# Weight blocks for the product scheme kept in device memory instead of being added up again, with earlier sums of y

## Chip, cores and metric

The kernel runs on one core of one Trainium2 chip. The metric is the device time of one execution in microseconds (us). Three runs of the kernel before gave 550.37, 550.64 and 551.04 us.

## What is computed

Two sequences of 768 tokens (8 heads of 64) go through a local-plus-summary attention; its output, 1536 x 512, goes through a maxout layer and then through a bilinear layer. All of it is f32.

```
a = softmax([scores in a window of 16 tokens | scores against 24 block maxima of k])
x = a @ [v | block means of v]                      # 1536 x 512
h = maximum(maximum(x @ w1, x @ w2), x @ w3)        # 1536 x 768
y = h @ w_out                                       # 1536 x 512
out = ((y @ w_a) * (y @ w_b)) @ w_out2              # 1536 x 1536 inside, 1536 x 512 out
```

## The kernel before

**Chunks and operands.** The tokens are four chunks of 384: chunks 0 and 1 are the first sequence, 2 and 3 the second. f32 accuracy comes from splitting every operand into a rounded high part and a low part (fp32r); `mm3` (L532) makes one product of three matmuls, high x high, low x high, high x low. A matmul here is 128 x 128 weights against 128 x 384 tokens. One block of weights is 128 x 512 (four such tiles), 24 matmuls for one pair of chunks.

**Weights.** A block arrives as 512 KB of 64-bit numbers (`w_load`, L434, issued by SyncE into the tiles `w64`), is rounded to f32 in the tile `w32` (`w_round`: ScalarE L454 and L456, VectorE L458 and L459, GpSimd L460) and split into the tile `wt` (`w_split` and `w_parts`: ScalarE L464 the high part, VectorE or GpSimd L465 the low part). `weights()` calls these steps ahead of use; `W64` and `ERA0` are numbers of load tiles and set how far ahead the loads go. The `w32` block is freed once it is split.

**The order of the program.** Attention of the first sequence, its maxout with the first 18 weight blocks (`ph`, evacuated by `evac`), its second product `layer2` (`py`, giving `y` by `halves`) with the attention of the second sequence woven in (`TURNS` says between which steps), then `pair1()`: the maxout of the second sequence. `pair1` takes pairs of column blocks (f, m), nine in all. Two at the start and one at the end are `plain` (eight products of 12 matmuls each, `ph`). The six between are made two at a time by `products()`, a scheme that forms a 2 x 2 block product from seven products instead of eight (`PRODUCTS`; PSUM tiles `hb`, `hg`, `hd`). It wants sums and differences of the blocks of weights, `s`, and of x, `xs`. `x_sums` makes those of x (GpSimd `xr<-x` L592, then VectorE and ScalarE). `w_sums(f, m)` makes those of the weights, six times: the `w32` blocks are gone, so GpSimd first adds high and low part of two blocks to full blocks `rc`

```
        for r, w in ((r0, w0), (r1, w1)):
            G.tensor_tensor(r, w[:, 0], w[:, 1], ALU.add)
        s12, s34 = sums4(*(r[:, o:o + 256] for r in (r0, r1) for o in (0, 256)))
```

then VectorE makes four 128 x 256 sums (`sums4`, L471 to L474) and ScalarE and GpSimd split them (L464, L465 `wt<-s`). `result` evacuates the products on VectorE: `pt<-hd,s` and the like (L633), `pt<-pt` (L635, a maximum of two SBUF tiles), `pt<-hb,pt` and `pt<-ph,pt` (L640). `layer2` of chunks 2 and 3 follows (`py<-hg`), and then layer 3 (`qb`, `qg`, `qd`; for both sequences by the same seven products) and layer 4 (`po`).

**Sums of y.** Layer 3 wants sums of y as well. `sums_of` makes them; for the first sequence that is 11 VectorE instructions of 128 x 768 (`yt<-y,yt` L745 and `yd<-y` L749, with `yt<-y` on ScalarE, L744). They are called at the steps `SUMS` of `pair1`. The first loads of layer 3's weights have to wait for a tile of h (the gate, `GATE`): GpSimd copies a column of it into each load tile (L433), and the load comes behind that; their rounding begins with `psw<-w` (L454) and `w<-psw` (L458). In layer 3, `ca<-qb,m` (L803) is VectorE's evacuation of a product.

**What sets the order.** SyncE issues its DMAs in the order of the code. The rows of the other engines are ordered by a scheduler from the order of the code and from pins (`behind_marks`, `behind_all`) that hold chosen work behind chosen evacuations. Every engine works its rows off in order. `XSUMS`, `WSUMS` and `ASK` say at which steps of `pair1` the sums of x and of the weights are called.

## Time and profile before

| | |
|---|---|
| median of 3 runs | 550.64 us |
| the profiled execution | 549.45 us |
| its span | 547.2 us |
| granted TensorE clock | 1.00 in every stretch, the 2.4 GHz level |
| TensorE matmuls busy | 534.0 us, 98% of the span, 3328 |
| VectorE (DVE) busy | 422.2 us, 77% |
| ScalarE (ACT) busy | 284.6 us, 52% |
| GpSimd (POOL) busy | 245.9 us, 45% |

The span is read as one long row of matmuls: what TensorE (PE) does not spend on them is 13 us, and the question at each place is what it waits for there. PEld is the loading of weights into TensorE, which shows waits most plainly. Rows give a start and a duration in us, and in brackets the idle time before with the instruction that ended it.

### The profile page before, as it was taken

Reading aid. Unit: us, or ns where it says so; the run is one execution under the profiler, and the core shown is the slowest. Engines: PE = TensorE matmul, PEld = TensorE weight load, DVE = VectorE, ACT = ScalarE, POOL = GpSimd, SP = SyncE. Lnnn points to the kernel's source line nnn. Section 1 sums busy time; section 2 is a strip of 40 time slices with the busy share of each in tenths; the row PEclk is TensorE's granted clock in tenths of the full one; section 3 lists DMA queues with packets and bytes.
Section 4 is the critical chain, followed back from the end, with each engine's and each line's share of the span. In section 5 each row is a group of like instructions: output and inputs, shape, how many; then the busy total and the mean of one; then the engine's idle time right before and its main releaser. Section 6 shows DMA issues by size and latency. Waiting matters only on the chain.

```text
span 547.2 us, 9042 instructions
## 1 busy us (share of the span) xinstructions
PE 534.0 (98%) x3328; PEld 506.3 (93%) x3328; DVE 422.2 (77%) x863; ACT 284.6 (52%) x692; POOL 245.9 (45%) x207
## 2 busy tenths in 40 slices
PE   7899999999999999999989999999999999999997
PEld 7789999999999999989989989989998998998986
DVE  5798985885439677699999997985997798574464
ACT  4699775676533342567667645633544543340130
POOL 3479997642239577544334342521621442230120
PEclk9999999999999999999999999999999999999999
DMA  8998334375100000232311241132122121000014
GB/s 297 356 278 294 123 116 151 110 223 165 38 1 1 2 0 1 106 97 107 116 48 68 78 153 40 40 115 78 38 78 78 40 77 40 1 0 1 0 49 183
DMA packets 17132, 51.82 MB, mean 95 GB/s; under 512 B 2112, under 2 KB 2752, under 8 KB 17088
## 3 DMA queue, kind: packets, MB, share of 16 engines
q1 hardware_dynamic: 17088, 51.25, 28.0%
q8 instruction: 26, 0.43, 0.3%
q14 instruction: 18, 0.15, 0.1%
HBM read 48.09 MB, written 3.15 MB: 94 GB/s over the span
## 4 chain that ended last, share of the span: by engine, by line
PE 80%; DVE 9%; POOL 4%; issue 2%; ACT 1%; DMA 1%; DVEq 0%; POOLq 0%; ACTq 0%
PE ph L532 17%; PE qb L532 16%; PE py L532 9%; PE qg L532 8%; PE po L843 6%; PE po L844 6%; PE po L842 6%; PE qd L532 4%; PE ps L261 3%; PE psv L318 2%; PE pst L299 2%; POOL wt L465 1%; DVE yt L745 1%; DVE yd L749 1%; DVE w L459 1%
## 5 line engine op out<-in xcount | busy, mean ns | idle before, releaser
L460 POOL TENSOR_TENSOR w<-w,w 128x512 int32<-128x512 int32 x60 | 85.3, 1431 | 140.5 <-DVE w L459 79.9
L532 PE MATMUL qb<-yt,wt 128*128 128x384 f32 x576 | 109.9, 336 | 1.7 <-DVE ca L803 1.3
L532 PE MATMUL ph<-x,wt 128*128 128x384 f32 x576 | 107.2, 338 | 0.0
L532 PEld LDWEIGHTS qb<-yt,wt 128*128 128x128 f32 x576 | 101.0, 188 | 3.5 <-DVE ca L803 1.6
L532 PEld LDWEIGHTS ph<-x,wt 128*128 128x128 f32 x576 | 99.1, 188 | 0.3
L810 POOL TENSOR_TENSOR t<-t,ca 128x384 f32<-128x384 f32 x36 | 43.7, 1226 | 67.5 <-DVE t L809 67.3
L532 PE MATMUL qg<-yt,wt 128*128 128x384 f32 x288 | 57.8, 335 | 0.5 <-DVE yt L745 0.5
L856 DVE TENSOR_TENSOR acc<-po,acc 128x512 f32<-128x512 f32 (+1 forms) x61 | 40.7, 678 | 22.3 <-PE po L844 22.2
L843 PE MATMUL po<-wt,hg 128*128 128x512 f32 (+1 forms) x146 | 56.6, 387 | 0.0
L844 PE MATMUL po<-wt,hg 128*128 128x512 f32 (+1 forms) x146 | 56.5, 387 | 0.0
L842 PE MATMUL po<-wt,hg 128*128 128x512 f32 (+1 forms) x146 | 56.5, 387 | 0.0
L532 PE MATMUL py<-hg,wt 128*128 128x384 f32 x288 | 54.0, 340 | 1.1 <-DVE pt L640 1.1
L532 PEld LDWEIGHTS qg<-yt,wt 128*128 128x128 f32 x288 | 50.6, 188 | 0.8 <-DVE yt L745 0.8
L532 PEld LDWEIGHTS py<-hg,wt 128*128 128x128 f32 x288 | 49.5, 188 | 1.6 <-DVE pt L640 1.4
L536 ACT ACTIVATE hg<-t 128x384 fp32r<-128x384 f32 x60 | 30.8, 521 | 34.7 <-POOL t L810 28.7
L268 ACT ACTIVATE s<-s,nm 128x120 f32<-128x120 f32 x96 | 36.9, 387 | 20.5 <-DVE nm L267 20.4
L456 ACT ACTIVATE w<-w 128x512 int32<-128x512 uint32 x60 | 39.4, 671 | 4.7 <-DMA w<-wall 4.7
L454 ACT ACTIVATE w<-w 128x512 f32<-128x512 f32 x30 | 20.3, 675 | 41.2 <-DMA w<-wall 41.1
L464 ACT ACTIVATE wt<-w 128x512 fp32r<-128x512 f32 (+1 forms) x60 | 34.7, 583 | 12.9 <-POOL w L460 11.9
L286 POOL TENSOR_TENSOR s<-s,r 128x720 f32<-128x720 f32 x16 | 22.2, 1390 | 42.6 <-DVE r L284 36.0
L465 DVE TENSOR_TENSOR wt<-w,wt 128x512 fp32r<-128x512 f32 (+1 forms) x44 | 33.7, 768 | 1.5 <-ACT wt L464 1.3
L537 DVE TENSOR_TENSOR hg<-t,hg 128x384 fp32r<-128x384 f32 x48 | 34.2, 722 | 0.9 <-ACT hg L536 0.8
(115 smaller groups left out, 990.1 us busy)
## 6 DMA issues: line engine op xcount, KB each, us to landing
w<-wall SPq DMA_DIRECT2D x60, 512.0 KB, 3.4
qv<-qt SPq DMA_DIRECT2D x15, 384.0 KB, 6.1
row<-kt SPq DMA_DIRECT2D x8, 416.0 KB, 3.6
full<-vt SPq DMA_DIRECT2D x8, 384.0 KB, 6.2
out<-acc SPq DMA_DIRECT2D x11, 256.0 KB, 2.0
qv<-vwin SPq DMA_DIRECT2D x12, 192.0 KB, 5.3
qv<-vwin SPq DMA_DIRECT2D x12, 96.0 KB, 5.0
qv<-qt SPq DMA_DIRECT2D x1, 256.0 KB, 4.5
```

Of the source, the lines that this page charges most:

```text
L268: A.activation(s[:, a], s[:, a], AF.Exp, bias=nm[:, a:a + 1], scale=-1.0, accum_out=sm[:, a:a + 1])
L456: A.activation(lw.bitcast(I32), lw, AF.Copy, scale=2.0 ** -29)
L460: G.tensor_tensor(w.bitcast(I32), w.bitcast(I32), lw.bitcast(I32), ALU.add)
L464: A.activation(w[:, 0], r, AF.Copy)
L465: eng.tensor_tensor(w[:, 1], r, w[:, 0], ALU.subtract)
L532: ins = T.matmul(ps, w[:, i, o:o + P], x[:, j], start=first and n == 0, stop=last and n == 2, skip_group_check=more).ins
L537: ins = eng.tensor_tensor(dst[:, 1], src, dst[:, 0], ALU.subtract).ins
L810: G.tensor_tensor(t, t, cs[c, f], ALU.mult)
L842: T.matmul(ps, g[:, 0], w[:, 0], start=(f == 0), stop=False)
L843: T.matmul(ps, g[:, 0], w[:, 1], start=False, stop=False)
L844: ins = T.matmul(ps, g[:, 1], w[:, 0], start=False, stop=(f == 1)).ins
L856: V.tensor_tensor(acc[c, i][:, cols_], ps, acc[c, i][:, cols_], ALU.add)
```

## The change

The twelve 128 x 512 blocks that `w_sums` rebuilds are instead written from `w32` to device memory when they are rounded (`spill`, a DMA by SyncE ahead of the next block's split), and loaded back from there into `rc` by SyncE. GpSimd's twelve adds go. Some numbers move with it: fewer load tiles (`W64` 6 to 4, `ERA0` 10 to 8), two instead of one for one pool of attention tiles (`FB`), the sums of y of the first sequence at steps 32, 36, 40, 44 instead of 40, 43, 46, 49 (`SUMS`), the sums of x and of the weights one to three steps later (`XSUMS`, `WSUMS`, `ASK`), and the attention of the second sequence ending one step of the first product's order sooner (`TURNS`).

```diff
--- before.py
+++ after.py
@@ -53,15 +53,16 @@
-W64, W32, WBUFS, QB, FB, SM, GB, BANKS = (6, 3), (4, 3), (24, 10), 4, (9, 1), 2, (12, 9), (2, 2, 1, 2, 2)
-GATE, ROOM, SUMS, EARLY34 = (2, 1), 16, (40, 43, 46, 49), 6
-PLAIN, XSUMS, WSUMS, WS, PT, MAX_G, LO_G, ASK = (2, 1), (2, 4), (5, 7), 8, 7, False, True, (0, 2)
-RING, LEAD, TURN, ERA0, ASKS, AHEAD, PRE, TURNS = 8, 5, (11, 2, 4), 10, (3, 4, 5, 7, 9), (4, 1), 3, ((6, N1 - 6, 6, 4, 4), (24, 34), (34, 43))
+W64, W32, WBUFS, QB, FB, SM, GB, BANKS = (4, 3), (4, 3), (24, 10), 4, (9, 2), 2, (12, 9), (2, 2, 1, 2, 2)
+GATE, ROOM, SUMS, EARLY34 = (2, 1), 16, (32, 36, 40, 44), 6
+PLAIN, XSUMS, WSUMS, WS, PT, MAX_G, LO_G, ASK, RC = (2, 1), (3, 5), (7, 8), 8, 7, False, True, (1, 3), 2
+SPILL = {3 * (2 * (j // 3) + i) + j % 3 for j in range(PLAIN[0], 9 - PLAIN[1]) for i in range(2)}
+RING, LEAD, TURN, ERA0, ASKS, AHEAD, PRE, TURNS = 8, 5, (11, 2, 4), 8, (3, 4, 5, 7, 9), (4, 1), 3, ((6, N1 - 6, 6, 4, 4), (24, 33), (33, 42))
@@ -93,6 +94,7 @@
     acc_p = ctx.enter_context(tc.tile_pool(name="acc", bufs=B * NT))
     sm_p = ctx.enter_context(tc.tile_pool(name="sm", bufs=SM))
     mo_p = ctx.enter_context(tc.tile_pool(name="mo", bufs=2))
+    spill_p = ctx.enter_context(tc.tile_pool(name="spill", bufs=1, space=bass.MemoryType.DRAM))
     ps_s = ctx.enter_context(tc.tile_pool(name="ps_s", bufs=BANKS[0], space=PSUM))
     ps_t = ctx.enter_context(tc.tile_pool(name="ps_t", bufs=BANKS[1], space=PSUM))
     ps_v = ctx.enter_context(tc.tile_pool(name="ps_v", bufs=BANKS[2], space=PSUM))
@@ -474,9 +476,14 @@
         V.tensor_tensor(s34[:, 256:512], a12, s12[:, 256:512], ALU.subtract)
         return s12, s34
+    spilled, spill = {}, []
     def w_split(q):
         kind, n, i = kinds[q]
         eng = V if SPLIT_DVE[era(q)][q % 3] else G
+        if q in SPILL:
+            spilled[q] = spill_p.tile([P, 512], F32, tag=f"spill{q}", name="spill")
+            spill.append((spilled[q], w32_t[q]))
         if kind in ("w", "o"):
             w_t[q] = w_parts(w32_t.pop(q), eng, "w" if kind == "w" else "w34")
         elif i == 0:
@@ -506,6 +513,9 @@
             ahead = min(AHEAD[0] + 2 * (w_done < ERA0 + 4), W64[w_done + AHEAD[0] > N12] - 2 * (w_done >= ERA0 + 4))
             for n, (step, more) in enumerate(((w_load, ahead), (w_round, AHEAD[1]), (w_split, 0))):
                 while w_at[n] < min(w_done + more, len(seq) if gate else N12):
+                    if step is w_split and spill:
+                        to, w = spill.pop()
+                        nc.sync.dma_start(out=to, in_=w)
                     step(w_at[n])
                     w_at[n] += 1
@@ -609,9 +619,9 @@
     def w_sums(f, m):
         w0, w1 = (w_t[3 * (f + i) + m] for i in range(2))
-        r0, r1 = (w32_p.tile([P, 512], F32, tag="rc", name="rc", bufs=2) for _ in range(2))
-        for r, w in ((r0, w0), (r1, w1)):
-            G.tensor_tensor(r, w[:, 0], w[:, 1], ALU.add)
+        r0, r1 = (w32_p.tile([P, 512], F32, tag="rc", name="rc", bufs=RC) for _ in range(2))
+        for i, r in enumerate((r0, r1)):
+            nc.sync.dma_start(out=r, in_=spilled[3 * (f + i) + m])
         s12, s34 = sums4(*(r[:, o:o + 256] for r in (r0, r1) for o in (0, 256)))
         eng = G if LO_G else V
         s12, s34 = (w_parts(x, eng, "ws") for x in (s12, s34))
```

In the rows of the order below, lines of the changed kernel up to L500 have numbers 2 higher, and those behind L540 have numbers 10 higher (L633 becomes L643, L640 L650, L745 L755, L749 L759, L532 L542); L518 is the write and L624 the load of a spilled block.

SyncE in the opening, behind a pair of window loads of attention (`vwin`): loads of weight blocks (`w<-wall`). Before:

```order
L434 DMA w_616<-wall 128x512
L434 DMA w_665<-wall 128x512
L434 DMA w_713<-wall 128x512
L434 DMA w_754<-wall 128x512
L434 DMA w_805<-wall 128x512
L434 DMA w_817<-wall 128x512
```

In the changed kernel behind the same pair (`spill<-w` is the write):

```order
L518 DMA spill<-w_560 128x512
L436 DMA w_713<-wall 128x512
L436 DMA w_755<-wall 128x512
L518 DMA spill<-w_670 128x512
L436 DMA w_808<-wall 128x512
L518 DMA spill<-w_718 128x512
L436 DMA w_822<-wall 128x512
L518 DMA spill<-w_760 128x512
L436 DMA w_929<-wall 128x512
L518 DMA spill<-w_813 128x512
L436 DMA w_958<-wall 128x512
L518 DMA spill<-w_827 128x512
```

Writes stand among the loads; each waits for the rounding of its own block, and what is behind it in the queue waits with it.

Behind the last window loads SyncE then issues the twelve loads of `rc` in one row, ahead of the first weights of layer 3, where before there is nothing. On GpSimd the twelve adds, which stood among and behind the eight `xr<-x`, are gone, and the eight stand together, with five `wt<-s` behind them.

VectorE, from the last evacuations of the second pair of products (`pt<-hb,pt`) into those of the third (`pt<-hd,s`). Before:

```order
L635 TENSOR_TENSOR pt<-pt 128x384
L474 TENSOR_TENSOR s<-rc,s 128x256
L640 TENSOR_TENSOR pt<-hb,pt 128x384 x2
L633 TENSOR_TENSOR pt<-hd,s_2847 128x384
L745 TENSOR_TENSOR yt<-y,yt 128x768
L633 TENSOR_TENSOR pt<-hd,s_2881 128x384
L745 TENSOR_TENSOR yt<-y,yt 128x768
L633 TENSOR_TENSOR pt<-hb,m_2902 128x384
L635 TENSOR_TENSOR pt<-pt 128x384
```

In the changed kernel:

```order
L755 TENSOR_TENSOR yt<-y,yt 128x768
L645 TENSOR_TENSOR pt<-pt 128x384
L650 TENSOR_TENSOR pt<-hb,pt 128x384
L645 TENSOR_TENSOR pt<-pt 128x384
L650 TENSOR_TENSOR pt<-hb,pt 128x384
L755 TENSOR_TENSOR yt<-y,yt 128x768
L759 TENSOR_TENSOR yd<-y 128x768
L755 TENSOR_TENSOR yt<-yd,yt 128x768
L643 TENSOR_TENSOR pt<-hd,s_2878 128x384
L643 TENSOR_TENSOR pt<-hd,s_2912 128x384
```

Four of the eleven instructions on y, 128 x 768 each, now stand ahead of `pt<-hd,s`, and none before. Behind them, from the first `pt<-hd,s` of the third pair to the first `ca<-qb,m` of layer 3, four instructions of 128 x 768 are fewer; on the way to the last `pt<-hb,pt` of `pair1` three of 128 x 256 (sums and a split of layer 3's weights) and one rounding of 128 x 512 have moved behind it, and a rounding `w<-psw` (L458, now L460) stands right behind the second `pt<-hd,s`. On TensorE that first `hd` now ends 11 matmuls further on in the order of `pair1`, the second one as far as before, and at the point where layer 3 needs `ca<-qb,m` six matmuls fewer stand ahead.

TensorE, the attention of the second sequence (`ps` scores, `pst` transposes, `psv` product with v) among the products `py`. Before:

```order
L261 MATMUL ps<-kept,qv 128x120 x4
L532 MATMUL py<-hg,wt 128x384 x6
L318 MATMUL psv<-aT,qv 64x64 x12
L299 MATMUL pst<-kept,s 120x128 x6
L261 MATMUL ps<-kept,qv 128x120 x2
L532 MATMUL py<-hg,wt 128x384 x3
L261 MATMUL ps<-kept,qv 128x120 x2
L532 MATMUL py<-hg,wt 128x384 x17
L318 MATMUL psv<-aT,qv 64x64 x12
```

In the changed kernel:

```order
L263 MATMUL ps<-kept,qv 128x120 x4
L542 MATMUL py<-hg,wt 128x384 x20
L320 MATMUL psv<-aT,qv 64x64 x12
L263 MATMUL ps<-kept,qv 128x120 x4
L542 MATMUL py<-hg,wt 128x384 x5
L301 MATMUL pst<-kept,s 120x128 x6
L542 MATMUL py<-hg,wt 128x384 x12
L263 MATMUL ps<-kept,qv 128x120 x4
L542 MATMUL py<-hg,wt 128x384 x3
L320 MATMUL psv<-aT,qv 64x64 x12
```

Fewer `py` stand between the parts of attention in places, and it ends sooner.

## Rows read from the trace of the kernel before

**Rows 1.** Stretches: us, busy PE PEld DVE ACT POOL, clock, DMA share, GB/s.

```profile
63.50:100.00 36.50, 36.50 (x212) 36.50 (x212) 28.41 (x45) 22.02 (x41) 31.19 (x26) 1.00 0.36 115
184.80:243.90 59.10, 57.39 (x326) 55.95 (x324) 44.71 (x74) 27.48 (x52) 38.80 (x32) 1.00 0.13 45
265.00:290.00 25.00, 23.11 (x130) 22.12 (x129) 22.80 (x45) 16.92 (x36) 8.95 (x5) 1.00 0.30 96
290.00:470.00 180.00, 180.00 (x949) 168.41 (x948) 157.00 (x263) 87.54 (x177) 62.92 (x50) 1.00 0.19 66
```

**Rows 2.** Waits of TensorE's weight loads from 170 to 295 us: total, times, longest.

```profile
PEld qb L532 <- DVE ca L803: 1.6, 1, 1.6
PEld py L532 <- DVE pt L640: 1.4, 1, 1.4
PEld hb L532 <- DVE pt L633: 0.9, 2, 0.6
PEld qg L532 <- DVE yt L745: 0.8, 1, 0.8
PEld hg L532 <- ACT wt L464: 0.7, 1, 0.7
PEld qb L532 <- DVE yt L745: 0.4, 1, 0.4
```

**Rows 3.** One weight block's 24 matmuls, from the chain that ended last: start, us.

```profile
186.95 4.17 PE ph L532 x24
```

**Rows 4.** The adds: ns minimum/median/maximum, first and last start.

```profile
L614 POOL TENSOR_TENSOR rc<-wt x12: 1277/1290/1597, 163.8 to 213.7; 128x512 f32<-128x512 f32 x12
```

**Rows 5.** VectorE's groups, 184.8 to 243.9 us: busy us, mean ns, idle before.

```profile
L635 DVE TENSOR_TENSOR pt<-pt 128x384 f32<-128x384 f32 x12 | 8.9, 743 | 0.0
L471 DVE TENSOR_TENSOR s<-rc 128x256 f32<-128x256 f32 x5 | 5.0, 1006 | 7.1 <-POOL rc L614 7.1
L749 DVE TENSOR_TENSOR yd<-y 128x768 f32<-128x768 f32 x2 | 1.9, 947 | 0.0
```

**Rows 6.** All of one sum on VectorE: ns minimum/median/maximum.

```profile
L471 DVE TENSOR_TENSOR s<-rc x6: 409/1018/1494, 166.9 to 218.0; 128x256 f32<-128x256 f32 x6
```

**Rows 7.** VectorE's timeline: start, us, instruction.

```profile
223.32 0.56 DVE L633 TENSOR_TENSOR pt<-hd,s 128x384 f32<-128x384 f32 x1
231.47 0.69 DVE L458 TENSOR_SCALAR w<-psw 128x512 uint32<-128x512 uint32 x1 [1.88 <-ACT psw L454]
243.35 0.55 DVE L640 TENSOR_TENSOR pt<-hb,pt 128x384 f32<-128x384 f32 x1
284.61 0.54 DVE L803 TENSOR_TENSOR ca<-qb,m 128x384 f32<-128x384 f32 x1
```

**Rows 8.** GpSimd's timeline: the copies that let the loads of layer 3's weights go.

```profile
226.44 1.16 POOL L433 COPY w<-hg 128x1 f32<-128x1 f32 x3
```

**Rows 9.** TensorE's timeline: start, us, matmuls, idle time before.

```profile
222.01 1.55 PE L532 MATMUL hd<-x,wt 128*128 128x384 f32 x8
243.95 23.17 PE L532 MATMUL py<-hg,wt 128*128 128x384 f32 x132 [1.06 <-DVE pt L640]
285.21 2.38 PE L532 MATMUL qb<-yt,wt 128*128 128x384 f32 x12 [1.31 <-DVE ca L803]
```

**Rows 10.** DMA issues of the page: KB each, median us from issue to landing.

```profile
w<-wall SPq DMA_DIRECT2D x60, 512.0 KB, 3.4
out<-acc SPq DMA_DIRECT2D x11, 256.0 KB, 2.0
```

**Rows 11.** DMA issues between 36 and 84 us.

```profile
w<-wall SPq DMA_DIRECT2D x15, 512.0 KB, 4.4
```

**Rows 12.** GpSimd's timeline: four roundings.

```profile
66.33 5.15 POOL L460 TENSOR_TENSOR w<-w,w 128x512 int32<-128x512 int32 x4
```

**Rows 13.** The chain that ended last: scores of the second sequence.

```profile
157.46 0.88 PE ps L261 x8
```

**Rows 14.** GpSimd's timeline: the normalisation behind these scores.

```profile
160.50 1.39 POOL L286 TENSOR_TENSOR s<-s,r 128x720 f32<-128x720 f32 x1 [7.53 <-DVE r L284]
```

## Prediction

> **What bounds the kernel now.** I first read the stretches of the span [rows 1]. From 63.5 to 100 us and from 290 to 470 us the matmuls fill every microsecond, at clock 1.00. No other engine's work there costs anything. The stretch from 184.8 to 243.9 us, where the six sums of weights are made and used, has 57.39 us of matmuls in 59.10, and the one from 265 to 290 us has 23.11 in 25.00. These are the places that this change can help. The waits of TensorE's weight loads from 170 to 295 us say on whom [rows 2]: 0.9 us for VectorE's `pt`, 0.7 for ScalarE's `wt` (a split of sums of weights), 1.4 for `pt` at the end of `pair1`, 0.8 and 0.4 for the sums of y, 1.6 for `ca`. That is 5.8 us, and it is the most that can be won here. Everything else is matmuls, and the change removes none.
>
> Then I looked at why VectorE is late. The twelve adds on GpSimd take 1.29 us each, and are spread from 163.8 to 213.7 us [rows 4]. VectorE sits idle 7.1 us for them [rows 5]. Also, it runs slowly beside GpSimd: a sum `s<-rc` takes 0.41 us at best but 1.01 in the mean of this stretch, and `pt<-pt` 0.743 us in the mean, where evacuations of the same size with an input from PSUM take 0.54 to 0.56 [rows 5 to 7].
>
> **The change part by part.**
>
> *The adds.* They are 12 x 1.29, 15.5 us of GpSimd, an engine that rows 2 do not name. What they give VectorE is the 7.1 us of idle time, and part of the slowness. Five of the first sums lose 1.01 - 0.41 = 0.6 us each and twelve `pt<-pt` 0.743 - 0.55 = 0.2, together 3.0 + 2.4 = 5.4 us [rows 5 to 7]. I take half of that, 2.7 us, as given back, since GpSimd's other work (`wt<-s`, `xr<-x`) stays; the bounds are none and all. So VectorE has 9.8 us more room ahead of the third pair of products, with bounds of 7.1 and 12.5.
>
> The Trainium skill bears on that half: "SBUF — State Buffer", section "Who interferes with whom", says that a VectorE instruction with two SBUF inputs contends with a GpSimd instruction that reads SBUF. The trace agrees (0.743 us in the mean for `pt<-pt`, against 0.55 with an input from PSUM). By this rule the splits `wt<-s` that stay go on slowing VectorE, which speaks against the change and for R1 below; if all the slowness went with the adds, the room would be 12.5 us and R1 would hang on ScalarE alone.
>
> *The writes.* Twelve DMAs of 256 KB. The nearest row is the write of `out`, 256 KB in 2.0 us [rows 10]. Most of them pass where the DMA share is 0.36 [rows 1], and TensorE waits for no write. Their cost is the queue: SyncE issues in order, and a write waits until its block is rounded, so the weight loads behind it do too. With fewer load tiles the loads run four blocks ahead. Four blocks are 4 x 4.17 = 16.7 us of TensorE [rows 3]. What has to fit in is a landing of 4.4 us [rows 11] and rounding and splitting, five or six instructions one after the other; with the longest row there, GpSimd's 5.15 / 4 = 1.29 us [rows 12], six of them are 7.7 us, together 12.1. That fits with 4.6 us to spare, so the cost is 0; it begins when a landing takes over 9.0 us.
>
> *The loads.* Twelve loads of 256 KB take no longer than a load of 512 KB, 3.4 us [rows 10], and stand behind attention's last window loads; the DMA share of that stretch is 0.13 [rows 1]. The first pair is there long before its sums. Later ones wait for a free `rc` tile, and that comes free with each sum on VectorE. Cost 0, and up to 3.4 us if the first is late.
>
> *The moved attention.* TensorE does the same matmuls. Between a score and the transpose behind it there are fewer products in places: I counted the matmuls in between, and the shortest gap falls from 5.95 to 5.19 us, at 4.17 / 24 = 0.174 us a matmul [rows 3] and attention's own ones as their rows have them. The chain to be hidden is scores at 157.46 to the end of the normalisation, 160.50 + 1.39 = 161.89, so 4.4 us from the start of the scores and 3.6 from their end [rows 13, 14]. Cost 0.
>
> *The sums of y and VectorE's order.* Now TensorE's waits one by one.
>
> A. `hb` and `hg`, 0.9 + 0.7 us. VectorE no longer waits for adds, but the last sums of weights still come late in its order, with about 1 us of slack. I take 1.1 of the 1.6 us as saved (bounds 0 and 1.6).
>
> B. `py`, 1.4 us. Four instructions on y now stand ahead of the third pair's `pt<-hd,s`, 0.95 us each [rows 5], 3.8 us. The 9.8 us of room take them up, so TensorE sets the time of `pt<-hd,s`. Before, the six matmuls of the first `hd` ended at 222.01 + 6 x 0.174 = 223.05 [rows 3, 9] and VectorE came at 223.32 [rows 7]. Now this `hd` is 11 matmuls later, 1.9 us, and A makes it 1.1 sooner: 223.85, so `pt<-hd,s` starts at about 223.9. From there to the `pt<-hb,pt` that `py` waits for it took 243.35 - 223.32 = 20.0 us. Three instructions of 0.41 and a rounding of 0.69 have gone from in between, 1.9 us. The wait for `psw`, 1.88 us of idle time [rows 7], shrinks: GpSimd's copies at 226.44 [rows 8] stood behind its splits and adds, and come sooner; I take 1.3 us (bounds 0 and 1.9). That makes 16.8 us, so `pt<-hb,pt` ends at 223.9 + 16.8 + 0.55 = 241.25. TensorE would be there at 243.95 - 1.4 - 1.1 = 241.45 [rows 2, 9]. All of the 1.4 us is saved, by a margin of 0.2 (bounds 0 and 1.4).
>
> C. `qg` and `qb` on the sums of y, 0.8 + 0.4. Four instructions on y have been done before: 1.0 saved (bounds 0 and 1.2).
>
> D. `ca`, 1.6 us. From `pt<-hd,s` to `ca<-qb,m` it took 284.61 - 223.32 = 61.3 us [rows 7]. Now four instructions on y are gone, 3.8 us, and 1.3 for `psw`: 56.2, so `ca` ends at 223.9 + 56.2 + 0.54 = 280.65. TensorE resumed at 285.21 [rows 9]; without its wait, the 3.5 us of A to C, and six matmuls that now stand behind this point (1.04), it would be there at 279.1. So it still waits 1.6, and D saves nothing. VectorE sets the time here: the gain is 285.21 - 280.65 - 1.04 = 3.5 us, which is also A + B + C (a small slip in these would change only how it divides).
>
> I take off 0.2 for small new waits behind this point and at `pt<-ph,pt`, behind which the second pair's first sums now stand: 3.3 us. The profiled execution's 549.45 us becomes 546.15; it stands 1.2 us below the median of the runs, 550.64, from which the same gain gives **547.3 us**. The bounds come from D's sum: with no gain at `psw` 2.2 us, with the slowness of VectorE gone too some 4.9 (the upper half of 5.4 us, 2.7, halved again for the half that lies ahead of 223.9), and never more than the 5.8 us of rows 2.
>
> **The rivals.**
>
> R1, VectorE stays the bound. The rounding that now stands right behind the second `pt<-hd,s` waits for `psw`, and everything behind it on VectorE waits too. If the copies do not come sooner, it starts at 231.47 as before [rows 7]. From it to `pt<-hb,pt` there are now six instructions on y, six roundings and splits and seven evacuations: at 0.95, 0.69 and 0.55 [rows 5, 7] 13.7 us, less 19 x 0.08 as starts overlap ends by that much, 12.1. `pt<-hb,pt` starts at 243.6, and `ca` ends at 284.61 + 0.25 - 1.9 + 0.54 = 283.5: a gain of 285.21 - 283.5 - 1.04 = 0.7 us, 549.9 us. For it: the copies stay behind the same low parts of h in GpSimd's order. Against: GpSimd has 15.5 us less to do ahead of them.
>
> R2, the other side: attention's chain no longer fits in its gaps. It decides when the chain from the last score to the normalisation's end is over 5.2 us. At some 7 us (with GpSimd's and VectorE's queues as full as elsewhere) five gaps in the denser order would be short by 0.44, 0.86, 1.81, 0.49 and 0.99 us, 4.6 in all; with 3.3 won elsewhere that is 1.3 us slower, 551.9. For it: GpSimd does one normalisation at a time, 1.39 us, among `hg<-t` and roundings, and the change moves these. Against: the chain is 3.6 us there now, and GpSimd sat idle 7.53 us before it [rows 14].
>
> R3, the change does not do what it says: the loads of `rc` come late, since SyncE issues them in order behind attention's window loads, and each waits for a tile. Then VectorE waits up to 3.4 us for a landing in place of the add, A to D stay but for some tenths, and it is 550.4. Against: SyncE has nothing else to issue in that stretch, and the first of the loads waits for no sum.
>
> **How the numbers follow.** The forecast has a chance of 0.67, R1 0.15, R2 0.10, R3 0.08. A measurement of this kernel can tell about 0.2%, 1.1 us: faster is below 549.5, slower above 551.7. Nearly all of the forecast counts as faster (0.64), and a third of R1 and R3 (0.08): 0.72. Their other two thirds, a little of R2 and a little of the forecast are the same: 0.18. Slower is most of R2, and a chain in the opening that I have wrong: 0.10. The range goes from 545.2, nearly all of the waits gone, to 550.4, which takes in R1 and R3 and leaves out R2.
>
> **What would show it.** No idle time of VectorE for `rc` from 184 to 224 us, and `s<-rc` near 0.41 us but for those beside `wt<-s`. The third pair's first `pt<-hd,s` near 224 us, GpSimd's copies at 223 to 225 instead of 226.44, the `w<-psw` behind the second `pt<-hd,s` at 228 to 230 and not at 231.5 (R1). Of the waits in rows 2 only that for `ca` left, 1 to 2 us long. TensorE as full as before from 63.5 to 171 us: if not, and it waits for a transpose or `psv`, R2 is right; if for a weight block, it is the queue in the opening. All loads of `rc` landed ahead of their sums (against R3). I would be wrong if a wait appeared ahead of 170 us, where I count the change at nothing.

## The result: slower, and the profile after

The changed kernel takes 556.63 us (median of 4 runs, 555.81 to 557.6) where the kernel before takes 550.5 on the same chip: a ratio of 1.0112, 95% interval 1.0093 to 1.0131. It is 6.1 us slower; the forecast was 3.3 us faster. The profiled execution took 556.72 us, with a span of 554.9 and a mean clock of 0.99.

The stretches of the kernel after, with the columns of [rows 1]:

```profile
63.50:100.00 36.50, 36.27 (x208) 35.95 (x209) 25.88 (x43) 22.67 (x42) 29.50 (x24) 1.00 0.72 237
184.80:243.90 59.10, 56.94 (x318) 56.27 (x317) 47.21 (x78) 28.52 (x53) 31.19 (x25) 0.97 0.27 87
243.90:265.00 21.10, 21.10 (x123) 21.10 (x123) 20.61 (x34) 16.27 (x31) 11.00 (x7) 1.00 0.38 141
265.00:290.00 25.00, 20.95 (x112) 19.56 (x111) 20.81 (x37) 14.66 (x31) 12.57 (x5) 0.95 0.07 21
290.00:470.00 180.00, 179.76 (x938) 168.33 (x937) 152.50 (x261) 86.67 (x178) 62.89 (x49) 0.99 0.22 71
```

The opening is nearly as before: 36.27 us of matmuls in 36.50, at a DMA share of 0.72 where it was 0.36. GpSimd's busy time from 184.8 to 243.9 us falls from 38.80 us [rows 1] to 31.19: the adds are gone. But TensorE does not gain from it: it has 56.94 us of matmuls there, at a clock of 0.97, and from 265 to 290 us only 20.95, at 0.95. Waits of its weight loads from 170 to 295 us (total, times, longest):

```profile
PEld qb L542 <- DVE ca L813: 3.8, 1, 3.8
PEld hb L542 <- DVE pt L643: 2.4, 1, 2.4
```

Four smaller ones, 0.5 to 0.6 us each, are for ScalarE. The waits for `wt`, `py` and `yt` [rows 2] are gone. The one for `ca` has grown from 1.6 to 3.8 us, and the one of `hb` from two short ones, 0.9 in all, to one of 2.4. TensorE's timeline shows both, and where layer 3 begins:

```profile
222.79 2.24 PE L542 MATMUL hd<-x,wt 128*128 128x384 f32 x12
235.80 3.63 PE L542 MATMUL hb<-xs,wt 128*128 128x384 f32 x12 [2.04 <-DVE pt L643]
243.72 25.12 PE L542 MATMUL py<-hg,wt 128*128 128x384 f32 x144
268.69 1.20 PE L542 MATMUL qb<-yt,wt 128*128 128x384 f32 x6
288.38 4.21 PE L542 MATMUL qb<-yt,wt 128*128 128x384 f32 x12 [3.50 <-DVE ca L813]
```

Twelve matmuls take 2.24 us where nothing disturbs them, and 3.63 and 4.21 behind the two waits. The clock column of short windows there says why:

```profile
235.80:239.40 3.60, 3.60 (x13) 3.60 (x14) 3.60 (x7) 1.28 (x3) 0.92 (x1) 0.60 0.45 139
288.30:292.50 4.20, 4.12 (x13) 4.12 (x14) 4.17 (x10) 0.49 (x1) 1.08 (x1) 0.50 0.41 126
292.50:294.50 2.00, 2.00 (x8) 2.00 (x7) 1.23 (x3) 0.98 (x2) 1.30 (x1) 0.50 0.02 6
```

Behind the waits TensorE runs at or near 0.50, the level of 1.2 GHz, for some 3 and 6 us. Layer 3's first matmul starts at 268.69 us; before it was 266.96:

```profile
266.96 1.20 PE L532 MATMUL qb<-yt,wt 128*128 128x384 f32 x6
```

So of the 7.7 us by which the span grew, 1.7 lie ahead of layer 3, and 6.0 behind.

**The first wait.** VectorE's timeline in `pair1` (brackets: idle time before, and what ended it), and GpSimd's:

```profile
194.22 0.56 DVE L643 TENSOR_TENSOR pt<-hd,s 128x384 f32<-128x384 f32 x1 [2.03 <-PE hd L542]
203.99 0.56 DVE L643 TENSOR_TENSOR pt<-hb,m 128x384 f32<-128x384 f32 x1 [2.02 <-PE hb L542]
210.09 0.56 DVE L643 TENSOR_TENSOR pt<-hd,s 128x384 f32<-128x384 f32 x1 [2.21 <-PE hd L542]
224.12 1.76 DVE L759 TENSOR_TENSOR yd<-y 128x768 f32<-128x768 f32 x1
226.85 0.98 DVE L755 TENSOR_TENSOR yt<-yd,yt 128x768 fp32r<-128x768 f32 x1 [0.96 <-ACT yt L754]
227.75 1.01 DVE L643 TENSOR_TENSOR pt<-hd,s 128x384 f32<-128x384 f32 x2
230.92 0.69 DVE L460 TENSOR_SCALAR w<-psw 128x512 uint32<-128x512 uint32 x1 [2.15 <-ACT psw L456]
235.20 0.54 DVE L643 TENSOR_TENSOR pt<-hb,m 128x384 f32<-128x384 f32 x1
```

```profile
223.50 3.27 POOL L547 TENSOR_TENSOR hg<-pt,hg 128x384 fp32r<-128x384 f32 x2 [1.99 <-ACT hg L546]
226.71 1.16 POOL L435 COPY w<-hg 128x1 f32<-128x1 f32 x3
271.52 9.34 POOL L462 TENSOR_TENSOR w<-w,w 128x512 int32<-128x512 int32 x2 [4.59 <-DVE w L461]
```

VectorE no longer waits for adds. It waits for products instead, 2.03, 2.02 and 2.21 us, in the first two pairs of products: the room became idle time there. Then come the four instructions on y, which take 0.95, 0.94, 1.76 and 0.98 us, with 0.96 us of waiting for ScalarE ahead of the last, and `pt<-hd,s` starts at 227.75, not near 224. The copies are at 226.71, as late as before [rows 8]; the `w<-psw` behind them at 230.92 [rows 7: 231.47]. Behind that stand instructions on y, and only then, at 235.20, `pt<-hb,m`, for which TensorE's `hb` has waited since 233.8. Before, VectorE came to it at 228.58, ahead of the rounding:

```profile
228.58 0.54 DVE L633 TENSOR_TENSOR pt<-hb,m 128x384 f32<-128x384 f32 x1
```

**The second wait.** The chain that ended last, ahead of layer 3's stall (start, us, what):

```profile
271.52 4.78 POOL w L462
276.39 2.85 issue
279.24 1.64 POOL w L462
280.89 3.32 DMA w<-wall
284.29 0.66 ACT w L456
```

and the timelines of ScalarE and VectorE at its end:

```profile
285.39 0.61 ACT L466 ACTIVATE wt<-w 128x512 fp32r<-128x512 f32 x1
```

```profile
286.11 0.69 DVE L467 TENSOR_TENSOR wt<-w,wt 128x512 fp32r<-128x512 f32 x1 [3.42 <-ACT wt L466]
287.78 0.55 DVE L813 TENSOR_TENSOR ca<-qb,m 128x384 f32<-128x384 f32 x1
```

Blocks are numbered in the order of their loads. Behind layer 2's last, 23, come 24 to 59, which are 24 blocks of layer 3 and 12 of layer 4; of 24 to 32, which the expectations below call layer 3's nine, 30 and 31 are layer 4's. Read from the bottom: `ca` stands behind the low part of block 31 on VectorE, for which VectorE sat idle 3.42 us until ScalarE had made the high part (285.39). In ScalarE's order that high part stands behind the rounding of block 35 (284.29), whose load went out at 280.89 us, when GpSimd's addition, the last step of the rounding of block 32, had let its load tile go. And this addition, 1.6 us long, stood on GpSimd behind that of block 31, which took 7.76 us from 271.52 us on ("issue" in the chain is the one waiting for the other). GpSimd's eight additions of this kind, all of one line between 250 and 296 us (ns minimum/median/maximum):

```profile
L462 POOL TENSOR_TENSOR w<-w,w x8: 1294/1530/7761, 252.6 to 293.0; 128x512 int32<-128x512 int32 x8
```

The one of 7.76 us is block 31's; 1.29 is the best. From 271.5 to 280.9 us VectorE is busy without a gap, nearly all of it with instructions on two SBUF inputs. The Trainium skill, "SBUF — State Buffer", section "Who interferes with whom", says that such an instruction contends with a GpSimd instruction that reads SBUF. The stretched addition agrees with that; no run here takes VectorE's instructions away to show it by itself.

### The profile page after: what moved, and what is told of

It is laid out like the page before. It is cut to its first block, busy times and chain, and to the rows that moved or that the text cites. A ratio compares the mean times of both kernels' runs of the same rounds, so it can differ in the third digit from the quotient of the medians.

```text
span 554.9 us, 9112 instructions
## 1 busy us (share of the span) xinstructions
PE 538.6 (97%) x3328; PEld 510.3 (92%) x3328; DVE 414.5 (75%) x863; ACT 284.1 (51%) x692; POOL 236.4 (43%) x195
## 4 chain that ended last, share of the span: by engine, by line
PE 74%; DVE 12%; DMA 6%; POOL 4%; ACT 2%; issue 2%; SPq 0%; POOLq 0%; DVEq 0%; ACTq 0%
PE ph L542 15%; PE qb L542 15%; PE qg L542 7%; PE po L854 6%; PE po L853 6%; PE po L852 6%; PE py L542 5%; PE qd L542 4%; PE ps L263 3%; PE hb L542 3%; POOL w L462 2%; DMA w<-wall 2%; DVE wt L467 2%; PE psv L320 2%; DMA qv<-vwin 2%
## 5 line engine op out<-in xcount | busy, mean ns | idle before, releaser
L462 POOL TENSOR_TENSOR w<-w,w 128x512 int32<-128x512 int32 x60 | 92.9, 1553 | 144.4 <-DVE w L461 88.4
L542 PE MATMUL qb<-yt,wt 128*128 128x384 f32 x576 | 112.3, 341 | 4.6 <-DVE ca L813 3.7
L542 PEld LDWEIGHTS qb<-yt,wt 128*128 128x128 f32 x576 | 102.6, 191 | 7.5 <-DVE ca L813 4.5
L542 PE MATMUL ph<-x,wt 128*128 128x384 f32 x576 | 105.7, 338 | 0.2 <-ACT x L546 0.2
L542 PEld LDWEIGHTS ph<-x,wt 128*128 128x128 f32 x576 | 99.7, 189 | 0.9 <-ACT x L546 0.5
L542 PE MATMUL qg<-yt,wt 128*128 128x384 f32 x288 | 58.5, 338 | 0.0
L542 PE MATMUL py<-hg,wt 128*128 128x384 f32 x288 | 53.6, 339 | 0.0
L542 PEld LDWEIGHTS qg<-yt,wt 128*128 128x128 f32 x288 | 51.5, 191 | 0.1
L542 PEld LDWEIGHTS py<-hg,wt 128*128 128x128 f32 x288 | 49.5, 188 | 0.1
L458 ACT ACTIVATE w<-w 128x512 int32<-128x512 uint32 x60 | 39.6, 667 | 2.7 <-DMA w<-wall 2.6
L467 DVE TENSOR_TENSOR wt<-w,wt 128x512 fp32r<-128x512 f32 (+1 forms) x44 | 30.9, 702 | 11.4 <-ACT wt L466 11.2
L547 DVE TENSOR_TENSOR hg<-t,hg 128x384 fp32r<-128x384 f32 x48 | 36.1, 758 | 1.1 <-ACT hg L546 0.9
```

The lines of the kernel that those rows point to most:

```text
L458: A.activation(lw.bitcast(I32), lw, AF.Copy, scale=2.0 ** -29)
L462: G.tensor_tensor(w.bitcast(I32), w.bitcast(I32), lw.bitcast(I32), ALU.add)
L467: eng.tensor_tensor(w[:, 1], r, w[:, 0], ALU.subtract)
L542: ins = T.matmul(ps, w[:, i, o:o + P], x[:, j], start=first and n == 0, stop=last and n == 2, skip_group_check=more).ins
L547: ins = eng.tensor_tensor(dst[:, 1], src, dst[:, 0], ALU.subtract).ins
```

## The experiments

All were timed in rounds beside the kernel before on the same chip, whose medians were 550.2 to 550.7 us there; a ratio is given with its 95% interval. The scheduler orders the rows of the engines anew with every edit, so a run shows an edit together with the order that comes with it. Three theories are named in the expectations. Y: the sums of y, moved ahead on VectorE. P: the rounding `w<-psw`, which waits for a gated load, ahead of `pt<-hb,m`. L: the rounding of layer 3's weights, held by loads and GpSimd, holds `ca`.

**1. The spilled blocks alone, and the sums of y alone.** `e1_spill_alone` is the kernel before with ten of the twelve blocks kept in device memory (the first pair of blocks is still added up on GpSimd) and every other number as before. `e2_sums_alone` is the kernel before with one number changed.

```diff
# e2_sums_alone, against before
-GATE, ROOM, SUMS, EARLY34 = (2, 1), 16, (40, 43, 46, 49), 6
+GATE, ROOM, SUMS, EARLY34 = (2, 1), 16, (32, 36, 40, 44), 6
```

> Ten of the twelve blocks go through device memory (the first sum of weights is still added up), and all the numbers are those of before. Theory Y (the sums of y moved ahead on VectorE cost the time): not slower than before, 547 to 550.5 us, no wait of TensorE over 1 us for the evacuation pt<-hb,m near 235 us. Theory P (VectorE's rounding w<-psw, which stands ahead of that evacuation here too, waits for the gated load): 553 us or more, with a wait of some 2 us there and the clock at half behind it. Theory D (the writes, loads and SyncE's queue cost): 553 us or more, with the loss ahead of 171 us or in waits for rc.

> The kernel before with the sums of y at 32, 36, 40, 44 and nothing else. Three sums of y now stand ahead of the third pair's pt<-hd,s and three behind it, and w<-psw stays behind pt<-hb,m. Theory Y: 553 to 557 us, a wait for pt<-hb,m or the like of 2 us or more in pair1. Theory P and theory D: 549.5 to 551.5 us.

Spill alone: 550.36 us, ratio 1.0002 (0.9987 to 1.0017), no change. Sums alone: 552.01, 1.0041 (1.0026 to 1.0055), slower, but by less than Y wants. In the spill alone `w<-psw` stands ahead of `pt<-hb,m` too (227.28 and 229.23 us), and TensorE's weight loads wait only 0.4 us for that: P, as a cost of this order alone, falls, and D with it. With the sums alone, GpSimd's copies come at 228.63 us, and VectorE's timeline has:

```profile
227.74 1.01 DVE L633 TENSOR_TENSOR pt<-hd,s 128x384 f32<-128x384 f32 x2
```

That is where the changed kernel has it, so the sums of y suffice to make it late. Layer 3 starts at 267.16 there, 0.2 us later than before; most of that run's loss lies behind it.

But behind the spill's zero there are two effects. Timelines of GpSimd, ScalarE and TensorE with the spill alone, one fence for each:

```profile
223.02 0.42 POOL L435 COPY w<-hg 128x1 f32<-128x1 f32 x3
```

```profile
278.97 0.63 ACT L466 ACTIVATE wt<-w 128x512 fp32r<-128x512 f32 x1 [3.08 <-POOL w L462]
```

```profile
283.48 3.85 PE L542 MATMUL qb<-yt,wt 128*128 128x384 f32 x12 [2.73 <-DVE ca L816]
```

The copies come at 223.02, 3.4 us sooner than before [rows 8], and layer 3 starts at 264.21 instead of 266.96. So the spill does win in `pair1` what its removal of adds promised. Then ScalarE waits 3.08 us for GpSimd's rounding, TensorE 2.73 for `ca`, and runs its next twelve matmuls in 3.85 us. All of it is given back.

**2. Other places for the sums of y, and attention as before.** All are the changed kernel with one line changed.

```diff
# e3_sums_later
-GATE, ROOM, SUMS, EARLY34 = (2, 1), 16, (32, 36, 40, 44), 6
+GATE, ROOM, SUMS, EARLY34 = (2, 1), 16, (36, 40, 43, 46), 6
# e7_sums_split
+GATE, ROOM, SUMS, EARLY34 = (2, 1), 16, (32, 36, 43, 49), 6
# e4_turns_back: the last two pairs of TURNS
-(24, 33), (33, 42)
+(24, 34), (34, 43)
```

> The changed kernel with the sums of y at 36, 40, 43, 46: two instead of four instructions on y ahead of the third pair's pt<-hd,s, w<-psw still ahead of pt<-hb,m. Theory Y: about half of the loss comes back, 551 to 554 us. Theory P and theory D: 555.5 to 557.5 us.

> The changed kernel with the sums of y at 32, 36, 43, 49: two instructions on y ahead of the third pair's pt<-hd,s instead of four, and one instead of three between it and pt<-hb,m. Theory Y for the wait in pair1 alone: the wait of 2 us for pt<-hb,m near 235 us is gone, and no other of that size takes its place before layer 3; what happens at ca is layer 3's own. 552.5 to 555.5 us. If w<-psw alone makes that wait: it stays, 556 to 557.5 us.

> The changed kernel with the attention of the second sequence placed as before. If the denser attention costs nothing, 555.5 to 557.5 us; if it is a part of the loss (rival R2 of the prediction), below 555 us, with the gain ahead of 171 us.

Later: 557.86 us, 1.0136 (1.0121 to 1.0152). Split: 559.9, 1.0168 (1.0153 to 1.0183). Attention as before: 555.96, 1.0103 (1.009 to 1.0116). The first two lie above every range that was expected. With later sums the wait of `hb` is gone, but `py` and then `qg` wait instead (with split sums, all three). Timelines of TensorE and ScalarE with later sums:

```profile
245.08 24.75 PE L542 MATMUL py<-hg,wt 128*128 128x384 f32 x132 [2.30 <-DVE pt L650]
284.71 1.33 PE L542 MATMUL qg<-yt,wt 128*128 128x384 f32 x3 [4.40 <-ACT m L803]
```

```profile
283.09 0.66 ACT L456 ACTIVATE w<-w 128x512 f32<-128x512 f32 x1 [5.37 <-DMA w<-wall]
```

So moving the sums part of the way back moves the waits and makes the kernel slower still: Y as it was put falls. The wait of `qg` is the chain of the second wait again: ScalarE's evacuation `m` of an earlier product stands behind a rounding that waits 5.37 us for a load. The attention order is worth 0.7 us at most, and the two intervals overlap: R2 is not the cause.

**3. Layer 3's rounding.** `e5_four_tiles` is the spill alone with one more load tile for layer 3 (four; five instead of six ahead of it). `e6_add_on_vector` is the changed kernel with a single addition, that of block 32, moved from GpSimd to VectorE. `e8_alone_add_on_vector` moves those of blocks 31 and 32 in the spill alone, and `e9_before_add_on_vector` the same two in the kernel before, as a control.

```diff
# e5_four_tiles, against e1
-W64, W32, WBUFS, QB, FB, SM, GB, BANKS = (6, 3), ...
+W64, W32, WBUFS, QB, FB, SM, GB, BANKS = (5, 4), ...
# e6_add_on_vector, against the changed kernel, in w_round
-        G.tensor_tensor(w.bitcast(I32), w.bitcast(I32), lw.bitcast(I32), ALU.add)
+        (V if q in (32,) else G).tensor_tensor(w.bitcast(I32), w.bitcast(I32), lw.bitcast(I32), ALU.add)
```

> As the kernel with the spill alone, but with four load tiles instead of three for the weights of layer 3 (and five instead of six for those before). Theory L (the rounding of layer 3's blocks, which waits for loads and for GpSimd, holds VectorE's ca up, and so the gain of 2.9 us at the start of layer 3 is lost again): the wait for ca falls from 2.7 us to under 1.5, the clock stays at the upper level behind it, 546.5 to 549 us. If the load tiles are not what holds it: 549.5 to 551 us.

> The changed kernel with the last addition of one rounding (the ninth block of layer 3, that which GpSimd began in the busiest stretch of VectorE) done by VectorE. Theory L with GpSimd held off by VectorE's instructions as the place: the next load is issued some 3 us sooner than at 280.9, the wait of 3.5 us for ca falls under 2 us, 552 to 554.5 us. If GpSimd's slowness there does not matter: 556 to 557.5 us.

> The spill alone with the last additions of the eighth and ninth block's rounding of layer 3 done by VectorE, which also puts two roundings behind ca<-qb,m instead of ahead of it. Theory L: the wait of 2.7 us for ca falls under 1.5 us, 546.5 to 549 us. Otherwise 549.5 to 551.5 us.

> The kernel before, with one edit: the last addition of the rounding of weight blocks 31 and 32 is made by VectorE instead of GpSimd. Nothing is kept in device memory here. It is the control of the run in which the same edit stood beside the blocks kept in device memory, 548.12 us. If the 2.4 us that were gained there belong to the edit alone (the wait of TensorE for ca, 1.6 us before, goes, and nothing else is needed), this gives 548 to 549. If they belong to the earlier products, which the edit only lets through layer 3's start, this is at most 1.6 us faster than before, 549 to 550.5, and the waits ahead of 243 us (0.9 us for pt, 0.7 for wt, 1.4 for py) stay.

The tile: 549.82 us, 0.9986 (0.9977 to 0.9995), a small gain, in the range for load tiles that are not what holds it; TensorE's weight loads still wait 2.3 us for `ca`. (In the spill alone ScalarE waits for the addition itself, as shown above, and not for a load.) The single addition in the changed kernel: 552.05, 1.0032 (1.0021 to 1.0043). That one edit takes 4.6 of the 6.1 us away; the wait of the weight loads for `ca` falls from 3.8 to 0.3 us, and `ca<-qb,m` starts at 283.69 instead of 287.78. The time is in theory L's range, but not by the way that was expected. Timelines of GpSimd and ScalarE in that run:

```profile
271.43 7.78 POOL L462 TENSOR_TENSOR w<-w,w 128x512 int32<-128x512 int32 x1 [4.59 <-DVE w L461]
```

```profile
281.16 0.62 ACT L466 ACTIVATE wt<-w 128x512 fp32r<-128x512 f32 x1
283.20 0.69 ACT L456 ACTIVATE w<-w 128x512 f32<-128x512 f32 x1 [1.42 <-DMA w<-wall]
```

GpSimd's slow addition is block 31's, was not the one moved, and takes 7.78 us here too; the next load goes out at 279.90, 1.0 us sooner where 3 was expected. What the edit changed is ScalarE's order: the high part of block 31 now stands ahead of the rounding of block 35 instead of behind it, at 281.16 instead of 285.39, and `ca` comes sooner by as much. Up to 278 us the order of every engine is that of the changed kernel, yet the twelve matmuls behind the wait of `hb` took 2.41 us at clock 1.00 in this profile, and layer 3 starts at 267.19. So 1.5 of the 1.7 us by which the changed kernel's layer 3 started late are the half clock of that one execution.

Two additions with the spill alone: 548.12, 0.9957 (0.9942 to 0.9972), faster than before. The same two in the kernel before: 552.58, 1.0043 (1.0025 to 1.0062), slower, and above both ranges. There new waits appear behind 290 us, where the kernel before has one of 0.6; weight loads from 290 us on:

```profile
PEld qb L532 <- ACT u L793: 1.8, 1, 1.8
PEld qd L532 <- DVE t L809: 1.2, 1, 1.2
PEld qb L532 <- DVE t L809: 1.0, 1, 1.0
```

So the gain of 548.12 is not the edit's own: beside the same edit the spilled blocks are worth 4.5 us (of which 1.9 is what the edit costs the kernel before), and without it nothing.

**4. More additions, and the control.** `e10_all_adds_on_vector` is the spill alone with the additions of the nine blocks 24 to 32 on VectorE; `e12_before_most_adds` the kernel before with eight (25 to 32); `e13_after_five_adds` the changed kernel with five (28 to 32). Each changes the same line:

```diff
# e10_all_adds_on_vector
+        (V if q in (24, 25, 26, 27, 28, 29, 30, 31, 32) else G).tensor_tensor(...)
# e12_before_most_adds
+        (V if q in (25, 26, 27, 28, 29, 30, 31, 32) else G).tensor_tensor(...)
# e13_after_five_adds
+        (V if q in (28, 29, 30, 31, 32) else G).tensor_tensor(...)
```

> The blocks kept in device memory alone, with all other numbers of the kernel before, and the last additions of the rounding of all nine blocks of layer 3 (24 to 32) on VectorE instead of only the last two. If what remains at layer 3's start is GpSimd, made slow by VectorE's instructions on two SBUF inputs, this is as fast as with two or faster, 547 to 548.2 us, with no wait for ca. If VectorE is the bound there, seven more instructions of 0.7 to 1.3 us ahead of ca bring the wait for ca back, 2 to 5 us, and it gives 550 to 553.

> The kernel before, with the last additions of the rounding of eight of layer 3's nine weight blocks (25 to 32) on VectorE, and nothing kept in device memory. It is the control of the run with all nine and the blocks kept in device memory, 545.79 us. If that gain of 4.9 us comes from the additions, this gives 546 to 548 us, with no wait for ca. If it comes from the blocks kept in device memory, and the additions only let it through layer 3's start, the waits ahead of 243 us stay (0.9 us for pt, 0.7 for wt, 1.4 for py), q begins where it does before, near 267 us, and the time is 549 to 552.5 us.

> The changed kernel with the last additions of the rounding of blocks 28 to 32 on VectorE (one of them alone gave 552.05 us). If GpSimd at layer 3's start were all that is wrong with the changed kernel, its blocks kept in device memory would now show as they do alone with nine additions moved, and it would give 546 to 548.5 us. If the order of pair1 with the sums of y sooner costs by itself, the wait of hb for the pt behind the rounding of psw stays, 1.5 to 2.1 us, layer 3 starts near 268 us instead of 264.2, and it gives 550.5 to 552.5.

Spill and nine: **545.79 us**, 0.991 (0.9895 to 0.9926), the fastest of all and below its range. Before and eight: 549.37, 0.9984 (0.9975 to 0.9993), as the second theory had it. Changed and five: 547.75, 0.9955 (0.9942 to 0.9968); its time is in the first range, but the wait of `hb` and layer 3's start, below, are what the second theory said. The stretch in which the changed kernel had 20.95 us of matmuls, with five additions moved in it, and with nine and the spill alone:

```profile
265.00:290.00 25.00, 25.00 (x146) 25.00 (x145) 24.11 (x50) 20.22 (x42) 2.63 (x2) 1.00 0.20 64
```

```profile
265.00:290.00 25.00, 25.00 (x146) 25.00 (x145) 23.38 (x49) 18.55 (x39) 3.53 (x3) 1.00 0.25 78
```

TensorE is full in both. Six additions on VectorE there take no longer than its other instructions of that size (ns minimum/median/maximum, spill and nine):

```profile
L462 DVE CUSTOM_DVE_ANT_0 w<-w,w x6: 677/681/684, 252.8 to 281.7; 128x1024 uint16<-128x1024 uint16 x6
```

With five additions moved in the changed kernel, the wait in `pair1` has stayed, with `w<-psw` at 231.34 us:

```profile
236.22 2.38 PE L542 MATMUL hb<-xs,wt 128*128 128x384 f32 x12 [1.89 <-DVE pt L643]
```

The start of layer 3 (its first `qb`) and what the span has left behind it, from the profiles, set the two parts apart:

| kernel | median | layer 3 starts | left of the span |
|---|---|---|---|
| before | 550.5 | 266.96 | 280.2 |
| changed | 556.63 | 268.69 | 286.2 |
| changed, one addition (e6) | 552.05 | 267.19 | 282.9 |
| changed, five additions (e13) | 547.75 | 267.56 | 277.8 |
| spill alone (e1) | 550.36 | 264.21 | 283.5 |
| spill alone, nine additions (e10) | 545.79 | 264.20 | 279.6 |
| before, eight additions (e12) | 549.37 | 268.23 | 279.6 |

The row of the changed kernel holds half clock, 1.5 us ahead of layer 3 and some 3 behind. Moving the additions, with the orders that come with it, shortens the last column: by 8.4 us in the changed kernel (3.3 already with one), 3.9 with the spill alone, 0.6 in the kernel before. What stands ahead of layer 3 decides the column before it: with the additions moved the spill wins 4.0 us there (268.23 to 264.20; 2.75 without, 266.96 to 264.21), and the rest of the change gives 3.4 back (264.20 to 267.56), of which 1.8 comes back behind (279.6 to 277.8).

**5. The copies sooner.** `e11_copies_sooner` is `e6_add_on_vector` with the low parts of h of two column blocks on VectorE.

```diff
-                split(h, t, V if f >= N2 - 2 and c == 3 else G)
+                split(h, t, V if f >= N2 - 2 and c == 3 or f in (2, 3) and c == 3 else G)
```

> The changed kernel with the addition of block 32 on VectorE, as in the run that gave 552.05 us, and the low parts of h of column blocks 2 and 3 of the last chunk made by VectorE instead of GpSimd, so that less of GpSimd's work stands ahead of the copies that let layer 3's weights load. The theory that the late copies are what is left (the rounding of the first of these weights stands on VectorE ahead of the pt that the product hb needs, and waits for its load): copies at or before 225 us instead of 226.9, the rounding by 229.5 instead of 230.9, the wait of hb falls from 1.9 to 1 us or less, and the time is 550 to 551.3. The theory that the sums of y that stand ahead of these evacuations are the cost, or that VectorE is full there: the two added instructions of 0.55 to 0.9 us on VectorE make up for the sooner copies, the wait of hb stays at 1.5 to 2.5 us, and it is 551.5 to 552.5.

552.43 us, 1.0034 (1.0021 to 1.0048): no better than `e6_add_on_vector`. The copies came only at 225.61 and `w<-psw` at 230.60; TensorE's timeline:

```profile
233.55 1.31 PE L542 MATMUL hb<-xs,wt 128*128 128x384 f32 x6 [0.60 <-DVE pt L643]
235.21 1.31 PE L542 MATMUL hb<-xs,wt 128*128 128x384 f32 x6 [0.35 <-DVE pt L643]
```

The wait of `hb` fell from 1.88 to 0.95 us, as P wants, but the time did not, as the other theory wants: small waits of `py` for `hg` and `pt` and a longer one for s took its place, and block 31's addition on GpSimd took 7.30 us. VectorE's order changed as well (a `yd<-y,yd` now stands ahead of `w<-psw`). It settles nothing on the time.

## Why the prediction was wrong

**Right.** The opening, the writes and the loads cost what was said: from 63.5 to 171 us TensorE has 107.27 us of matmuls in 107.50. The loads of `rc` took 2.9 us in the median from issue to landing and nobody waited for them: R3 is false. From 63.5 to 171 us the new waits of TensorE's weight loads are 0.5 us for x, at 65 us, and 0.2 in attention: R2 is false. The adds' idle time on VectorE is gone, and the first sums of weights fell to 0.73 us in the mean from 1.01 [rows 5], where near 0.41 was forecast. Term A was right in size up to the third pair's `hd`: its last matmul, as far on in the order as before, ended at 225.03 instead of 226.24 us, 1.2 sooner, and 1.1 was forecast. The wait of `hb` that it counted as mostly gone came back behind that, larger (step B). The slowness of VectorE gave back about 1.0 us instead of 2.7: six first sums won 0.28 each, but twelve `pt<-pt` took 0.803 us in the mean, more than the 0.743 [rows 5].

**Wrong, step B:** "The 9.8 us of room take them up, so TensorE sets the time of `pt<-hd,s`". The room was there, but not where the four instructions on y stand. VectorE works in order, and its room came out as 6.3 us of idle time ahead of evacuations that wait for products, at 194, 204 and 210 us. The instructions on y stand behind later evacuations and could not fill it. `pt<-hd,s` started at 227.75, 3.85 us later than the 223.9 forecast; the four and the wait for ScalarE among them stand right ahead of it. The sum had them at 3.8 us and filled by the room; they took 4.6 and 0.96, and the room had gone. The copies came at 226.71 and not 1.3 us sooner, since the low parts of h in front of them come out of evacuations that now stand among the instructions on y. That it is the order and not the spill is shown by two runs: with the spill alone the copies come at 223.02, and with the sums of y alone `pt<-hd,s` starts at 227.74 and the copies come at 228.63.

**Wrong, R1's price.** R1 was this mechanism: `w<-psw` behind the second `pt<-hd,s`, waiting as long as before. It started at 230.92; R1 said 231.47. But R1 was followed only to `pt<-hb,pt` and `ca`: from the rounding to `pt<-hb,pt` it took 12.1 us, as R1 had it (13.7 less 19 x 0.08 is 12.2 there, a slip of 0.1). The product that needs its input first is `hb`, by way of `pt<-hb,m`, which moved from 228.58 to 235.20 and was not followed. So R1 gave a gain of 0.7 us where layer 3 in fact started 1.7 us later (0.2 at full clock, `e6_add_on_vector`). `py` has no wait only because TensorE is late for it.

**Wrong, step D:** "56.2, so `ca` ends at 223.9 + 56.2 + 0.54 = 280.65". It ended at 287.78 + 0.55 = 288.33, 7.7 us later: 3.85 from B, and 3.8 because the way from `pt<-hd,s` to `ca` took 60.0 us. 3.42 of these are VectorE's idle time for ScalarE, at the end of the chain from GpSimd's addition by the load tile, the load and ScalarE's rounding. The sum took the way as before less what had been moved, and had no term for ScalarE, which works in order too, nor for GpSimd behind `pair1`. That the larger part lies in this chain is shown by `e6_add_on_vector`, 4.6 of the 6.1 us, and by `e13_after_five_adds`, with which the changed kernel is 2.6 us faster than the kernel before. Of its links, ScalarE's order is shown to suffice for the wait of `ca`: in `e6_add_on_vector` the addition of block 31 was as slow as before. What a fast addition would give in the old order no run shows.

**Not in the sum:** TensorE's half clock behind longer waits, some 3 and 6 us in the profile. What it costs in the median stays open: the profiled run had a mean clock of 0.99, the other three 0.997, with times from 555.81 to 557.6. In the profile it costs 1.5 us at the first wait and some 3 at the second. A slower TensorE also gives VectorE time to catch up, so the clock's loss and the waits can replace each other.

**What stays open:** how much of the 3.4 us ahead of layer 3 is P's single rounding and how much is VectorE full with the sums of y. `e11_copies_sooner` was to tell and didn't; the spill alone shows that the rounding's place costs little when its load comes in time. The changed numbers of load tiles and steps of the sums of x and of weights were not tried one by one. That VectorE's two-input instructions stretch GpSimd's addition is argued from the trace, not isolated.

## What to carry to other kernels

Room on an in-order engine counts only for instructions that stand where the room falls: look for what the engine will wait for next in the place of the wait removed, before spending the room. When an instruction that waits is moved ahead of evacuations, follow every one of them to the first matmul that needs it, not only the last. And a gain on one stretch is only passed on if the next stage's inputs are ready sooner too: the spilled blocks were worth nothing alone and 3.6 to 4.5 us beside the same additions on VectorE (nine against eight in the first case), so try such an edit together with what it runs into. Last, where a scheduler orders the rows, compare the order of all engines before crediting an edit: by its profile, the one that won 4.6 us did so by a row of ScalarE that changed places, not by the speed of the instruction that it moved.

## What the runs showed of the hardware that was not expected

- A GpSimd addition of 128 x 512 int32 takes 1.29 us at best and took up to 7.78 us beside a VectorE that was busy without a gap (`e6_add_on_vector`; 7.76 in the changed kernel). The same addition on VectorE took 0.68 us in most cases, and 1.34 in `e6_add_on_vector`.
- The clock's fall does not follow from the length of a wait alone. TensorE's timelines of `e4_turns_back` and of `e6_add_on_vector`, at the same place and with the same matmuls before it from 176 us on:

```profile
235.52 3.91 PE L542 MATMUL hb<-xs,wt 128*128 128x384 f32 x12 [1.86 <-DVE pt L643]
```

```profile
235.82 2.41 PE L542 MATMUL hb<-xs,wt 128*128 128x384 f32 x12 [1.88 <-DVE pt L643]
```

Waits of 1.86 and 1.88 us: behind the one, twelve matmuls took 3.91 us (granted clock 0.56 from 235.5 to 239.4 us, mostly the level of 1.2 GHz), behind the other 2.41 (1.00, the level of 2.4 GHz).
